# Block-sparse attention and a SoLU feed-forward: mask rows written into K^T and Q^T, and solu centred before the second matmul

## The chip, the cores and the metric

The kernel runs on one core of one Trainium2 chip. The metric is device time in microseconds (us) of one execution. A core has five engines with a queue each: TensorE (PE; its weight loads are PEld), VectorE (DVE), ScalarE (ACT), GpSimd (POOL) and SyncE (SP), which here only issues DMAs. Sixteen DMA engines serve all queues.

## What is computed

```python
# q, k, v: [4, 8, 768, 64];  blocks of 32, 24 of them, 3 sampled per row of blocks
scores = q @ k.T / sqrt(64)
mask = |blk_i - blk_j| <= 1, or block 0 or 23 on either side, or blk_j sampled for blk_i
attn = softmax(where(mask, scores, -1e9)) @ v
x = attn with the 8 heads side by side            # [3072, 512]
h = x @ w_in                                      # [3072, 1024]
solu = h * softmax(h)
ln = (solu - mean(solu)) / sqrt(var(solu) + 1e-6) * g_ln
out = ln @ w_out                                  # [3072, 512]
```

## The kernel before

**Units.** The work is cut into four batches. A batch has four pairs of heads and three tiles `t` of 256 queries. `prepare` brings K and Q of a pair into the forms kT and qT, with the 64 values of a head on the partitions and 768 tokens along the row; `attend` does one pair and one tile; `feed` does one tile of 256 tokens of the feed-forward in two halves of 128 tokens, so there are 48 calls of `attend` and 24 halves of feed.

**The mask.** The mask is part of the score matmul. Below the 64 rows of a head, kT has 24 rows that tell the block of each key, and qT has 24 rows that hold a large negative number for each block the query may not see. A score matmul therefore contracts over 88 rows. Before the change, these 24 values are put beside the 64 of each token in `kb` and `qb` (L356 to L365), and go through the transposes with them: `oneh` is built on POOL (L323), transposed on PE into `selq` (L329, L333), multiplied with `maskq` (L343, L348), and the product is copied to the three `qb` buffers (L365).

**Batch 0** is transposed on TensorE: a cast to bf16 (L441, L443), twelve transposes of 128x128 for the two heads of a pair (L458), one copy per head out of PSUM (L468, L470). **Batches 1 to 3** are cast on POOL (L417), transposed by a DMA (L422) and copied into kT and qT by DVE (L427); kT and qT have two buffers each, and the mask rows of the second are copied from the first by four DMAs (L643).

**attend.** Three steps of four score matmuls (L493), one exp each on ACT over 128x1024 (L500), then pv matmuls (L510) into one of two small PSUM banks (mbank), a reciprocal (L521) and the normalisation into x (L524).

**feed.** x is transposed by DMA (L554; the last tile on PE, L540). Per half: eight matmuls with w_in (L565), exp with its sum on ACT (L574), the product h * e on DVE (L577), the statistics (L580, L583), 1/sqrt on POOL (L585 to L590), a DMA transpose of the product (L598), eight matmuls with w_out (L605), the scaling (L615) and the store (L621). The mean is not subtracted from solu: w_out is centred instead. It is first scaled by g (L385), its column sums are formed on PE (L391) and brought to `wbar` (L396), and a second pass writes `w_out * g - wbar` (L398).

**Loads.** SP issues K, Q and V of the pairs in order, w_out (L379) and g (L382, one element per piece) after batch 0's, then the batches that follow. w_out in fp32 is held in the still unused parts of kT, qT and `eso` until it is scaled. w_in goes on POOL's queue (L375), since it is cast on the way, once the third V has landed.

**Order.** All instructions are first entered as operations with an engine, a duration, what they depend on, the buffers they take and a due time. `Plan.run` then places them: an engine takes, of what can start, the operation with the lowest due time. The due times of the units are in the tables A, F and Q, which are shifted by SHIFT. The order that comes out is fixed; each engine runs its own list in order and waits where something is late.

Of the kernel before, what the change touches and what calls it, by code (L numbers as in the profile page):

```python
# [7 lines left out]
FP32 = mybir.dt.float32  # L8
# [45 lines left out]
class Plan:  # L54
# [24 lines left out]
    def run(self):  # L79
# [10 lines left out]
        while len(order) < len(self.ops):  # L90
# [20 lines left out]
            if o.load is not None and o.xbar:  # L111
                self.xbar_free = max(self.xbar_free, t + 1.0) + o.load * (1.4 if self.dma_free > t + 1 else 1.0)
                self.dma_free = max(self.dma_free, t) + o.load
                o.seen = self.xbar_free + 1.3
            elif o.load is not None:
                self.dma_free = max(self.dma_free, t + 1.0) + o.load
                o.seen = self.dma_free + 1.3
                self.landed.append(self.dma_free)
                if len(self.landed) > 6 and o.eng == "SP":
                    self.free["SP"] = max(t + o.us, self.landed[-7])  # L120
# [20 lines left out]
def kernel(  # L141
# [14 lines left out]
    BLK = 32  # L156
# [47 lines left out]
    seb = bufs("se", [P, 1], FP32, 3)  # L204
    bnb = bufs("bn", [P, 2, 6], FP32, 3)
# [4 lines left out]
    wbar = const.tile([P, d_model], FP32, name="wbar")  # L210
# [10 lines left out]
    for nm, n in (("sh", 3), ("m", 2), ("kst", NST), ("qst", NST), ("vst", NST), ("kb", NKB), ("qb", NKB),  # L221
                  ("ex", NEX), ("x", NX), ("xT", NXT), ("e", NE), ("so", NSO), ("soT", NSOT), ("ot", NOT),
                  ("r", 2), ("se", 3), ("bn", 3), ("mv", 3), ("rs", 3), ("dq", 3)):
# [17 lines left out]
    def xbar_us(tiles):  # L241
# [7 lines left out]
        in_=bass.AP(tensor=_t32, offset=0, ap=[[2 * NR, NB], [1, 2 * NR]])), due=-100, load=0.01)  # L249
    warm = const.tile([1, 1], FP32, name="warm")  # L250
# [35 lines left out]

    def warm_mm(o):
        for _ in range(8):
            nc.tensor.matmul(bank(o)[:, 0:P], onesf, onesf, start=True, stop=True)

    for i in range(4):
        w = op("PE", 0.85, warm_mm, [m1], due=-60, take="m", after=[w] if i else [])
        w.last_of.append((w, "m"))
        w.held["m"][0] = 1


    oneh = const.tile([P, NCH, NB], BF16, name="oneh")
# [3 lines left out]
    kbf = const.tile([NB, NB], FP32, name="kbf")  # L301
    samp_f = const.tile([NB, NR], FP32, name="samp_f")
# [9 lines left out]
    def sel(t, us, fill, base, cm, pat, cmp=ALU.is_ge):  # L312
# [10 lines left out]
    ohs = chain(lambda o: nc.gpsimd.memset(oneh, 1.0),  # L323
                [sel(oneh, 0.3, 0.0, 0, NCH, [[1, NCH], [-BLK, NB]]),
                 sel(oneh, 0.3, 0.0, BLK - 1, -NCH, [[-1, NCH], [BLK, NB]])], -95)

    def selq_tr(o):
        for c in range(NCH):
            nc.tensor.matmul(bank(o, BF16)[0:NB, c * P : (c + 1) * P], oneh[:, c, :], ident, is_transpose=True,  # L329
                             start=(c == 0), stop=(c == NCH - 1))  # L330

    sqt = op("PE", 0.5, selq_tr, [ohs, mids], due=-88, take="m")
    sqs_ = op("DVE", dve_us(S, 2), lambda o: nc.vector.tensor_copy(  # L333
        out=selq.rearrange("b c p -> b (c p)"), in_=bank(sqt, BF16)[0:NB, 0:S]), [sqt], due=-88, last_of=[sqt])
    kbc = op("DVE", 0.2, lambda o: nc.vector.tensor_copy(out=kbf, in_=kbi), [io], due=-90)
    sf = op("DVE", 0.2, lambda o: nc.vector.tensor_copy(out=samp_f, in_=samp_i[:, :, 0]), [samp_dma], due=-90)
    last = op("DVE", 0.2, lambda o: nc.vector.tensor_scalar(  # L337
        out=anyeq, in0=kbf, scalar1=samp_f[:, 0:1], scalar2=None, op0=ALU.is_equal), [kbc, sf], due=-89)
    for r in range(1, NR):
        last = op("DVE", 0.2, lambda o, r=r: nc.vector.scalar_tensor_tensor(  # L340
            out=anyeq, in0=kbf, scalar=samp_f[:, r : r + 1], in1=anyeq, op0=ALU.is_equal, op1=ALU.max),
            [last], due=-89)
    mq = op("DVE", 0.2, lambda o: nc.vector.scalar_tensor_tensor(  # L343
        out=maskq, in0=anyeq, scalar=1.0, in1=static, op0=ALU.subtract, op1=ALU.mult), [last, stat], due=-88)

    def mask_mm(o):
        for c in range(NCH):
            nc.tensor.matmul(bank(o)[:, c * NB : (c + 1) * NB], selq[:, c, :], maskq, start=(c == 0),  # L348
                             stop=(c == NCH - 1))

    mmm = op("PE", 0.3, mask_mm, [mq, sqs_], due=-88, take="m")
    filled = {"k": [], "q": []}
    for i in range(NKB):
        for nm, t in (("k", kb), ("q", qb)):
            e = "DVE" if i == 0 else "POOL"
            z = op(e, 0.35, lambda o, t=t, i=i, e=e: (nc.vector if e == "DVE" else nc.gpsimd).memset(  # L356
                t[i][:, :, :, DM:].bitcast(I32), 0), due=-95 if i == 0 else -60,
                   after=[] if i == 0 else [mq])
            if nm == "k":
                f = op(e, 0.4, lambda o, i=i, e=e: (nc.vector if e == "DVE" else nc.gpsimd).tensor_copy(  # L360
                    out=kb[i][:, :, :, D:DM],
                    in_=oneh.rearrange("p (o c) b -> p o c b", o=1).broadcast_to([P, 2, NCH, NB])),
                    [ohs], due=-91 if i == 0 else -60)
            else:
                f = op("DVE", 0.4, lambda o, i=i: nc.vector.tensor_copy(  # L365
                    out=qb[i][:, :, :, D:DM],
                    in_=bank(mmm)[:, 0 : NCH * NB].rearrange("p (o c b) -> p o c b", o=1, c=NCH)
                    .broadcast_to([P, 2, NCH, NB])), [mmm], due=-87 if i == 0 else -39 + i,
# [326 lines left out]
```

## Time and profile before

| | |
|---|---|
| Time, median of 6 runs | 217.53 us (215.57 to 218.77) |
| The profiled execution | 217.16 us, its span 215.4 us |
| Granted TensorE clock, mean | 0.992 |
| PE busy | 201.1 us, 93% |
| ACT busy | 164.8 us, 77% |
| DVE busy | 148.8 us, 69% |
| POOL busy | 61.5 us, 29% |
| First score matmul | 8.66 us |
| Last exp of attention ends | 175.8 us |
| Last w_out matmul ends | 211.3 us |

The span runs from the first to the last instruction; the time of the execution has a little more around it. Busy shares are means over stretches with different limits, so they are read by stretch. A matmul counts as busy until its results are out, and matmuls overlap, so the work of TensorE is better counted in matmuls times the interval at which they follow each other.

### The profile page before, as it was taken

The page shows a single profiled execution, that of the slowest core. Times are in us where ns is not written, and L with a number is a line of the kernel's source. Part 1 is how long each engine was busy: PE and PEld are TensorE (multiplying, and loading weights), DVE is VectorE, ACT ScalarE, POOL GpSimd, SP SyncE. Part 2 cuts the span into 40 slices and gives each one's busy share as a digit, 9 for nine tenths or more (in the row PEclk, how much of TensorE's full clock was granted, in tenths as well). Part 3 has the DMA queues.
Part 4 walks back from the last instruction along what each step waited for, and adds up shares of the span by engine and source line. Part 5 has one row for each costly group of instructions (what it writes and reads, how often), then busy time and mean ns, then how long its engine had stood idle before and what let it go on. Part 6 is the DMA issues. An engine that isn't in the chain of part 4 may idle for free.

```text
span 215.4 us, 5758 instructions
## 1 busy us (share of the span) xinstructions
PE 201.1 (93%) x2284; PEld 141.7 (66%) x2284; DVE 148.8 (69%) x321; ACT 164.8 (77%) x198; POOL 61.5 (29%) x139
## 2 busy tenths in 40 slices
PE   7889977889999999999999999999999999999972
PEld 6667855567676688777777767777677764445530
DVE  7886554895886854467663867573858668999872
ACT  3489889389989899999999999899997982322300
POOL 7141014015154353132622241211301202231040
PEclk9999999699999999999999999999999999999999
DMA  5999999599999999999999998751312934968322
GB/s 182 324 378 335 248 283 174 165 214 254 216 303 190 245 239 241 249 282 213 328 147 281 225 296 212 144 138 36 97 48 53 114 85 115 215 147 187 122 102 97
DMA packets 73536, 42.66 MB, mean 198 GB/s; under 512 B 56420, under 2 KB 68708, under 8 KB 73508
## 3 DMA queue, kind: packets, MB, share of 16 engines
q1 hardware_dynamic: 72944, 41.24, 81.1%
q0 software_dynamic: 528, 1.05, 2.6%
q8 instruction: 18, 0.29, 0.6%
q14 instruction: 10, 0.08, 0.1%
q10 hardware_dynamic: 36, 0.00, 0.0%
HBM read 23.07 MB, written 6.29 MB: 136 GB/s over the span
## 4 chain that ended last, share of the span: by engine, by line
PE 75%; DMA 13%; DVE 5%; ACT 3%; issue 1%; POOL 1%; DVEq 0%; POOLq 0%; ACTq 0%
PE sbank L493 23%; PE mbank L605 18%; PE sbank L565 18%; PE mbank L510 13%; DMA kst<-in_k_dram 7%; ACT ex L500 3%; DMA kb<-kb 3%; DMA qb<-qb 2%; PE sbank L458 1%; DVE kT L470 1%; DVE anyeq L337 1%; DVE ot L615 1%; DVE eso L577 1%; PE mbank L540 0%; POOL kb L417 0%
## 5 line engine op out<-in xcount | busy, mean ns | idle before, releaser
L500 ACT ACTIVATE ex<-sbank 128x1024 bf16<-128x1024 f32 x144 | 137.7, 1034 | 10.9 <-PE sbank L493 9.1
L493 PE MATMUL sbank<-qT,kT 88*128 88x256 bf16 x576 | 85.5, 274 | 2.3 <-ACT ex L500 1.1
L493 PEld LDWEIGHTS <-kT 88*128 88x128 bf16 x576 | 53.2, 97 | 27.7 <-issue 5.1
L565 PE MATMUL sbank<-w_in_sb,xT 128*128 128x512 bf16 x192 | 52.6, 383 | 0.1
L510 PE MATMUL mbank<-va,ex 128*128 128x65 bf16 x1152 | 48.5, 194 | 2.6 <-DVE x L524 2.6
L510 PEld LDWEIGHTS <-ex 128*128 128x128 bf16 x1152 | 46.1, 98 | 7.3 <-issue 3.0
L605 PE MATMUL mbank<-w_out_sb,eso 128*128 128x512 bf16 x192 | 49.0, 379 | 1.1 <-DVE ot L615 1.1
L574 ACT ACTIVATE eso<-sbank 128x1024 bf16<-128x1024 f32 x24 | 24.9, 1036 | 21.9 <-issue 9.7
L577 DVE TENSOR_TENSOR eso<-sbank,eso 128x1024 bf16<-128x1024 f32 x24 | 29.2, 1217 | 6.6 <-ACT eso L574 6.2
L521 DVE RECIPROCAL r<-mbank 128x4 f32<-128x4 f32 x48 | 8.3, 176 | 34.7 <-PE mbank L510 34.5
L580 DVE BATCH_NORM_STATS2 bn<-eso 128x6 f32<-128x512 bf16 x48 | 30.6, 679 | 0.0
L605 PEld LDWEIGHTS <-eso 128*128 128x128 bf16 x192 | 17.7, 98 | 16.3 <-issue 1.2
L565 PEld LDWEIGHTS <-xT 128*128 128x128 bf16 x192 | 18.3, 99 | 11.5 <-issue 1.0
L587 POOL TENSOR_SCALAR mv<-se,mv 128x1 f32<-128x1 f32 x24 | 6.5, 272 | 64.3 <-DVE mv L583 57.6
L615 DVE TENSOR_SCALAR ot<-mbank,rs 128x512 f32<-128x512 f32 x24 | 17.8, 741 | 4.9 <-PE mbank L605 2.6
L476 POOL CAST va<-vst 128x768 bf16<-128x768 f32 x16 | 13.3, 832 | 26.5 <-PE mbank L510 14.4
L524 DVE TENSOR_TENSOR x<-mbank,r 128x256 bf16<-128x256 f32 x48 | 19.9, 419 | 1.0
L590 POOL TENSOR_TENSOR rs<-mv,neg_half 128x1 f32<-128x1 f32 x24 | 13.2, 549 | 5.9 <-DVE ot L615 4.2
L417 POOL CAST kb<-kst 128x768 bf16<-128x768 f32 x12 | 9.9, 824 | 14.0 <-DMA kst<-in_k_dram 14.0
L585 POOL TENSOR_TENSOR se<-se 128x1 f32<-128x1 f32 x24 | 4.7, 197 | 28.7 <-ACT eso L574 28.6
L417 POOL CAST qb<-qst 128x768 bf16<-128x768 f32 x12 | 10.2, 848 | 8.2 <-DMA qst<-in_q_dram 6.7
L427 DVE COPY kT<-kb 64x768 bf16<-64x768 bf16 x24 | 8.8, 366 | 5.1 <-DMA kb<-kb 4.8
(67 smaller groups left out, 90.0 us busy)
## 6 DMA issues: line engine op xcount, KB each, us to landing
vst<-in_v_dram SPq DMA_DIRECT2D x16, 384.0 KB, 5.1
out_dram<-ot SPq DMA_DIRECT2D x24, 256.0 KB, 2.9
kst<-in_k_dram SPq DMA_DIRECT2D x15, 384.0 KB, 5.6
qst<-in_q_dram SPq DMA_DIRECT2D x15, 384.0 KB, 4.9
w_in_sb<-in_moe_w_in_dram POOLq DMA_DIRECT2D x1, 1024.0 KB, 13.4
kT<-in_moe_w_out_dram SPq DMA_DIRECT2D x1, 768.0 KB
qT<-in_moe_w_out_dram SPq DMA_DIRECT2D x1, 768.0 KB
eso<-in_moe_w_out_dram SPq DMA_DIRECT2D x1, 512.0 KB, 16.9
```

Source lines behind the costliest of these rows:

```text
L417: nc.gpsimd.tensor_copy(out=half(cb[o.slot], 0).rearrange("p (c h d) -> p c h d", c=NCH, h=2), in_=st[ld.slot].rearrange("p h c d -> p c h ...
L476: vc = op("POOL", pool_us(S) + 0.3, lambda o: nc.gpsimd.tensor_copy(out=va[i][:, 2 * pr : 2 * pr + 2, :, 0:D], in_=vst[ld.slot]), [ld, von ...
L493: nc.tensor.matmul(s[:, m, :], kT[i][0:DM, pr, hh, jc * P : (jc + 1) * P], qT[i][0:DM, pr, hh, t * TW : (t + 1) * TW], start=(m % 2 == 0), ...
L500: exs.append(op("ACT", act_us(1024), lambda o, so=so: nc.scalar.activation(out=exb[o.slot], in_=sbank[so.slot], func=ACT.Exp, scale=scale) ...
L510: nc.tensor.matmul(acc[:, qt, hh, :], exb[exs[n].slot][:, m, qt * P : (qt + 1) * P], va[i][:, 2 * pr + hh, jc, :], start=(n + m + qt == 0) ...
L524: nrm = op("DVE", 0.39, lambda o: nc.vector.tensor_tensor(out=xb[x_of[(b, t)].slot][:, :, 2 * pr * D : (2 * pr + 2) * D].rearrange("p a (h ...
L565: nc.tensor.matmul(h[:, f * 512 : (f + 1) * 512], xTb[xp.slot][:, a, c, :], w_in_sb[:, c, f * 512 : (f + 1) * 512], start=(c == 0), stop=( ...
L574: se = op("ACT", act_us(d_ff) + 0.22, lambda o, h0=h0: nc.scalar.activation(out=eb[o.slots["e"]], in_=pair(h0), func=ACT.Exp, accum_out=se ...
L577: so = op("DVE", 1.19, lambda o, h0=h0, se=se: nc.vector.tensor_mul(out=sob[o.slot], in0=pair(h0), in1=eb[se.slots["e"]]), [se], due=F[a] ...
L580: bn = op("DVE", 2 * 0.64, lambda o, so=so: [nc.vector.bn_stats(out=bnb[o.slot][:, f], in_=sob[so.slot][:, f * 512 : (f + 1) * 512]) for f ...
L605: nc.tensor.matmul(bank(o0 or o), sotb[st.slot][:, f, :], w_out_sb[:, f, :], start=(f == 0), stop=(f == KF - 1))
L615: nc.vector.tensor_scalar(out=otb[o.slot], in0=bank(o0), scalar1=rsb[rs.slot], scalar2=None, op0=ALU.mult)
```

## The change

It does five things.

1. **Mask rows.** `selq` is built directly on POOL with 24 partitions and 768 columns. One PE operation of two matmuls forms the mask rows of Q for all 768 tokens. They are written to partitions 64 to 87 of kT and qT: for pair 0 by DVE and ACT, for the pairs 1 to 3 by one DMA each for kT and qT on POOL's queue, which repeats the rows of pair 0. `kb` and `qb` hold no mask columns any more. Batch 1's copies of the rows (the DMAs of L643) wait for the rows alone and no longer for pair 0's finished K^T and Q^T.
2. **Batch-0 transposes.** In pairs 1 to 3 both heads of a pair stand side by side, 128 columns, so six transposes serve two heads; they go to the small banks (`m`) instead of the score banks. In pair 0 each head keeps its own six, of 64 columns.
3. **Centring.** h * e also gives its sum over the row (`mu`); a new DVE instruction rewrites the product in place as `1024 * product - sum`. The statistics, the transpose and the matmul with w_out then use this, and eps is scaled by 1024 squared. The column sums, `wbar` and the second pass over w_out fall away.
4. **g** is loaded by ACT's queue as 8 rows of 128 and turned by one small matmul.
5. **w_in** is issued once the third K has landed, with a due time ahead of everything on POOL.

The planner's model of a DMA on POOL's queue is new, the four blocks of eight warming matmuls become seven of four, and the tables A, F, Q and SHIFT have new numbers, so the order of all the work differs.

```diff
-    ohs = chain(lambda o: nc.gpsimd.memset(oneh, 1.0), ...
-    sqt = op("PE", 0.5, selq_tr, [ohs, mids], due=-88, take="m")
+    sqs = chain(lambda o: nc.gpsimd.memset(selq, 1.0),
+                [sel(selq, 1.05, 0.0, 0, -BLK, [[1, NCH], [NCH, P]]),
+                 sel(selq, 1.05, 0.0, BLK - 1, BLK, [[-1, NCH], [-NCH, P]])], -93)
...
     def mask_mm(o):
-        for c in range(NCH):
-            nc.tensor.matmul(bank(o)[:, c * NB : (c + 1) * NB], selq[:, c, :], maskq, start=(c == 0),
-                             stop=(c == NCH - 1))
+        for g in range(2):
+            nc.tensor.matmul(sbank[o.slot].rearrange("p a b -> p (a b)")[0:NB, g * 512 : g * 512 + S // 2], maskq,
+                             selq.rearrange("b c p -> b (c p)")[:, g * (S // 2) : (g + 1) * (S // 2)],
+                             start=True, stop=True)
...
+        rows["k"].append(op("DVE", 0.3, lambda o, hh=hh: nc.vector.tensor_copy(
+            out=kT[0][D:DM, 0, hh, :], in_=selq.rearrange("b c p -> b (c p)")), [sqs], due=-2087 if hh == 0 else -60))
...
+    rest = {nm: op("POOL", 0.84, lambda o, t=t: nc.gpsimd.dma_start(
+        out=t[0][D:DM, 1:NPR].rearrange("p a h q -> p a (h q)"),
+        in_=t[0][D:DM, 0:1].rearrange("p a h q -> p a (h q)").broadcast_to([NB, NPR - 1, 2 * S])),
+        rows[nm], due=-2059, load=0.8) for nm, t in (("k", kT), ("q", qT))}
...
     w_in_load = op("POOL", 0.82, lambda o: nc.gpsimd.dma_start(
-        out=w_in_sb, in_=moe_w_in.rearrange("(c p) f -> p c f", p=P)), [stage[("v", 0, 2)]], due=-10, load=6.0)
+        out=w_in_sb, in_=moe_w_in.rearrange("(c p) f -> p c f", p=P)), [stage[("k", 0, 2)]], due=-2000, load=6.35)
...
-    g_load = op("SP", 0.45, lambda o: nc.sync.dma_start(
-        out=g_sb, in_=moe_g_ln.rearrange("(c p) -> p c", p=P)), due=-43.1, load=0.8, after=w_out_load)
+    g_load = op("ACT", 0.1, lambda o: nc.scalar.dma_start(
+        out=g8, in_=moe_g_ln.rearrange("(c p) -> c p", p=P)), due=-99.5, load=0.01)
+    gt = op("PE", 0.1, lambda o: nc.tensor.matmul(bank(o)[:, 0:KF], g8, identf[0:KF, 0:KF], start=True, stop=True),
+            [g_load, idf], due=-60, take="m")
...
-    wo = [op("DVE", 0.66, lambda o, c=c: nc.vector.scalar_tensor_tensor(
-        out=w_out_sb[:, c, :], in0=w_out_f[c], scalar=g_sb[:, c : c + 1],
-        in1=wbar, op0=ALU.mult, op1=ALU.subtract), [wb], due=28) for c in range(KF)]
+    wo = [op("DVE", 0.39, lambda o, c=c: nc.vector.tensor_scalar(
+        out=w_out_sb[:, c, :], in0=w_out_f[c], scalar1=g_sb[:, c : c + 1], scalar2=None,
+        op0=ALU.mult), [w_out_load[c // 3], gc], due=26) for c in range(KF)]
...
-            so = op("DVE", 1.19, lambda o, h0=h0, se=se: nc.vector.tensor_mul(
-                out=sob[o.slot], in0=pair(h0), in1=eb[se.slots["e"]]), [se], due=F[a] + 3, take="so",
+            so = op("DVE", 1.29, lambda o, h0=h0, se=se: nc.vector.scalar_tensor_tensor(
+                out=sob[o.slot], in0=pair(h0), scalar=1.0, in1=eb[se.slots["e"]], op0=ALU.mult,
+                op1=ALU.mult, accum_out=mub[o.slots["mu"]]), [se], due=F[a] + 3, take=("so", "mu"),
+            ce = op("DVE", 0.35, lambda o, so=so: nc.vector.tensor_scalar(
+                out=sob[so.slot], in0=sob[so.slot], scalar1=float(d_ff), scalar2=mub[so.slots["mu"]],
+                op0=ALU.mult, op1=ALU.subtract), [so], due=F[a] + 3, last_of=[(so, "mu")])
...
-    SHIFT = {"score": -851.13, "hmm": -451.93, "outp": 381.49, "pv": -264.97}
+    SHIFT = {"score": 17.85, "hmm": -42.86, "outp": 468.14, "pv": 80.68}
```

## The prediction

> **What bounds the kernel now.** I read the page's busy shares and slices first, then the chain that ended last, then a table by stretches, then the timeline where the table shows a loss.
>
> ```profile
> PE 201.1 (93%) x2284; PEld 141.7 (66%) x2284; DVE 148.8 (69%) x321; ACT 164.8 (77%) x198; POOL 61.5 (29%) x139
> PEclk9999999699999999999999999999999999999999
> PE 75%; DMA 13%; DVE 5%; ACT 3%; issue 1%; POOL 1%; DVEq 0%; POOLq 0%; ACTq 0%
> ```
>
> TensorE sets the end, but one slice has a low clock (the 6), and 13% of the chain are transfers, all early. The stretches:
>
> ```profile
> 0.00:8.60 8.60, 6.21 (x68) 5.23 (x69) 6.90 (x20) 2.51 (x4) 5.08 (x27) 1.00 0.73 219
> 8.60:24.00 15.40, 13.86 (x209) 12.17 (x209) 9.51 (x22) 14.02 (x16) 3.50 (x4) 1.00 1.07 346
> 24.00:36.30 12.30, 10.66 (x148) 8.07 (x145) 8.00 (x19) 10.69 (x12) 2.63 (x3) 1.00 1.17 221
> 36.30:48.00 11.70, 8.56 (x99) 6.21 (x99) 9.98 (x19) 7.29 (x10) 1.78 (x3) 0.85 0.85 199
> 48.00:177.40 129.40, 129.01 (x1600) 94.63 (x1598) 84.02 (x197) 122.30 (x144) 40.03 (x77) 1.00 0.88 194
> 177.40:212.20 34.80, 32.77 (x169) 15.35 (x167) 30.35 (x48) 8.00 (x16) 8.46 (x25) 1.00 0.54 138
> ```
>
> Columns: stretch, length, PE, PE loads, DVE, ACT, POOL busy, clock, DMA share, GB/s. Since a busy PE is not a full one, I price its work by the chain's pieces: score (L493) 0.44 us for 4, so 0.11; pv (L510) 0.75 for 24, so 0.031; feed (L565, L605) 0.86 for 4, so 0.215; a transpose of L458 0.83 for 12, so 0.069. From 48.0 to 206.0 the trace counts 448 scores, 920 pv, 184 + 177 feed matmuls: 49.3 + 28.8 + 77.6 = 155.7 us in 158.0. TensorE is full there, so whatever is gained or lost before 48 us moves the end by as much. From 36.3 to 48 it does 27 scores, 64 pv, 8 feeds = 6.7 us in 11.7: **5.0 us are lost**. Before that, exps pace it (ACT 14.02 of 15.4 and 10.69 of 12.3). The loss in the timeline:
>
> ```profile
> 37.24 0.79 DVE L427 COPY kT<-kb 64x768 bf16<-64x768 bf16 x2 [2.85 <-DMA kb<-kb]
> 38.15 0.42 DVE L524 TENSOR_TENSOR x<-mbank,r 128x256 bf16<-128x256 f32 x1
> 38.63 0.72 PE L510 MATMUL mbank<-va,ex 128*128 128x65 bf16 x16 [2.39 <-DVE x L524]
> 40.30 1.02 ACT L500 ACTIVATE ex<-sbank 128x1024 bf16<-128x1024 f32 x1 [2.94 <-PE sbank L493]
> ```
>
> VectorE stands in order behind a copy that waits for batch 1's first K transpose; the normalisation behind it holds a PSUM bank, TensorE waits 2.39 us, its granted clock then falls to half (L493 x4 takes 0.85 instead of 0.44, L565 x8 2.28 instead of 1.73). The x8 L398 passes (39.2 to 46.9) keep w_out unfinished, so no L605 runs before 54.
>
> **The change, part by part** (saving negative).
>
> *A. Mask rows and first score.* Now maskq is ready at 5.98, then six L348 matmuls, L365 0.45, transposes, L470 0.55, first score 8.66. After: two 384-column matmuls (0.16 each, by a feed's 512 columns at 0.215), about 0.2 of waits, an ACT copy like L468 (0.80), 0.1: 1.4 us behind the later of maskq and selq. selq is built on POOL: by the rows of 24 and 144 elements (memset 0.108 and 0.208, select 0.195 and 0.336) 768 elements cost 0.63 and twice 1.07, 2.8 us, against 3.0 us taken off POOL (oneh, its copies, zero fills). So it is ready at about 5 to 5.5, first score 6.6 to 7.4 on data that landed at 3.8. Bounds -2.0 and +0.5 (maskq held to 7.5); I take -1.2. DVE gains three row copies (0.37 each, by L427's 768 columns) and loses L333 1.12, three L365 of 0.45 and 0.75 of fills: hidden.
>
> *B. Batch-0 transposes and column sums.* Three pairs need 12 instead of 24 transposes: 36 x 0.069 = 2.5 us of PE. L391's 8 x 0.215 = 1.7 us and ACT's 0.60 go. But exps pace 8.6 to 36.3, and ACT is idle there only 3.0 us. Two of its gaps stand behind such work (0.98 before 25.72, 0.55 before 30.96). I take -1.0; bounds 0 and -3.0. The copies of 64 partitions still move 768 columns (0.55), free of cost against before. Transposes now take the two mbanks that pv uses; the freed score bank covers this, and if it doesn't, each collision costs one copy, 0.55, inside the bound of 0.
>
> *C. w_out in one pass.* L398 (5.8 us) and the wait for the whole column sum go; w_out is usable when L385's eight (0.48 each) are done, about 34 instead of 46.9. L605 and batch 1's later mask rows are released 12 us earlier, and DVE's order in 36 to 48 is empty enough that x isn't held. g's 1,024 pieces of 4 bytes leave the SP queue (landing 16.3 us, L385 waits 2.3 for it) for 8 rows on ACT's, 0.63 us of issue before the table load, hidden since q lands at 3.75; one small matmul and two DVE copies (0.2 each) bring g into place while w_out is on its way. What stays is that K of batch 1 comes through full DMA queues (share 1.07, 1.17), so I take -3.5 of the 5.0; bounds -5.0 and 0.
>
> *D. Queues.* The mask rows of three pairs become two POOL transfers of 216 KB. L643's like (96 packets of 3 KB) took 1.5 us of all engines; 144 take 2.2, g's give back 0.65, so w_out and K of batch 1 land 1.5 later. I hide this behind the 36 exps of batch 0 (36 x 0.94 = 34 us from 7.5, to 41); without that cover +1.5. On POOL, va's casts stand behind the rows' waits (to about 7.5); pv needs va at 13.2, so that is hidden. w_in's issue (14.71) moves to K of pair 2 (cast at 13.53), 1.2 us sooner; the 1 MB still ends with w_out near 28, first needed at 41. It costs nothing.
>
> POOL's transfers start late: w_in, issued by 15.69, shows its first packet at 19.15, 3.4 us later. The Trainium skill, SBUF — State Buffer, "SBUF: two separate sides", says that while a VectorE op in a two-port mode runs, GpSimd cannot write the descriptors of its DMAs, which speaks against sending rows this way in the stretch with most casts; it would put pair 1's rows behind two of VectorE's copies of 0.55 and make the sum 1.1 us worse, an estimate. By the trace alone rows issued at 7.5 to 8 land at 12 to 14, and pair 1 is needed after six exps, at 13.2: 0 to +1, I take 0.
>
> *E. Centring, 24 times on DVE.* L577 (1.217) becomes a scalar_tensor_tensor with a sum. L398's like takes 0.742 for 512, so 1.275 for 1,024; reading the sum out has no row on DVE, ACT's takes 0.212, so 0 to 0.21: +0.06 to +0.27, I take +0.18. The centring of 1,024 bf16: below, L427's copy of 768 (0.366) gives 0.43; above, L615's pace (0.741 for 512 from PSUM) gives 1.27; nearest is L385, 0.48. Together **+0.66 per tile** (0.49 to 1.54). In 48 to 177 DVE has 45 us free and takes 16 x 0.66 = 11: no cost. From 177.4 to 212.2 eight tiles run beside 30.35 busy in 34.8: 8 x 0.66 = 5.3 against 4.45 free, +0.85, and the last tiles' chain (exp, product, centring, transpose) is about 0.6 longer where TensorE already waits 1.11 for L615. I take **+2.0**; bounds +0.3 and 8 x 1.54 - 4.45 = +7.9.
>
> The Trainium skill, VectorE: DVE Perf Modes, "Two Vector instructions with no wait between them", has an op that writes out its accumulator as two instructions; no row of DVE here shows the second.
>
> **Sum:** -1.2 - 1.0 - 3.5 + 0 + 2.0 = -3.7 on a span of 215.4: 211.7. The profiled execution took 217.16, 1.8 around its span, and lies 0.37 below the median 217.53: predicted median 213.8.
>
> **Rivals.**
> 1. *The early gain is lost to DMA* (no change, 218.8): K of batch 1 (landing now at 30.1, then 6.0 of transpose) comes 1.5 later, TensorE waits for it as before, C is worth 0: -2.2 + 1.5 + 2.0 = +1.3. For it: the 13% of DMA in the chain. Against: only 28 exps had run by 37.4, so 8 of batch 0's 36 were left as cover.
> 2. *VectorE becomes the bound of the tail* (slower, 221.5): the centring takes L615's pace, +1.54 per tile, +7.9 at the end; against it stand A, B and, with VectorE behind from the start, half of C, -3.95: +3.95. Place: 177 to 212; it decides from (4.45 + 3.95 + 2.2) / 8 = 1.3 per tile, 2.2 being 1%. For it: DVE is 87% busy there. Against: L385's 0.48.
> 3. *The full early gain* (209.5): C -5.0, B -2.0, A -1.5, E +0.5 = -8.0.
>
> **Numbers.** Forecast 0.46, rival 1 0.22, rival 2 0.14, rival 3 0.18. A measurement here tells 1%, 2.2 us, from no change. Faster takes rival 3, nearly all of the forecast's 0.46 and a little of rival 1: 0.67; within 1% 0.19; slower 0.14. The range 209.0 to 219.0 holds all but rival 2's upper part and rival 3's edge; the forecast's own is 211.5 to 215.5.
>
> **What would show it.** Right: first score near 7.2; no half clock near 40; L605 before 48; PE full from about 40; a new bf16 line of 24 at 0.45 to 0.5; DVE above 95% from 177 on with TensorE gaps of 1 to 2 us. Wrong: the centring above 1 us, ACT waiting for pair 1's rows at 12 to 15, or batch 1's first score later than 39.

## The result and the profile after

The change made almost no difference: 217.47 us median (213.9 to 220.32, 40 runs) against 217.43 us for the kernel before in the same comparisons (82 runs). The ratio of the times is 0.9944, 95% interval 0.9919 to 0.9968; it counts of each kernel only the fast runs, those not over 1.5% above its fastest (12 of the kernel after), so it lies below the ratio of the two medians, and gains are given both ways where the two differ. The forecast was 213.8, a gain of 1.7%; by the ratio a third of that is there, by the medians nothing. The profiled execution took 217.81 us, its span 216.1, its clock 0.984.

The page of the kernel after, with the lines that answer to the first ones of before: busy time, clock, and the chain that ended last.

```profile
PE 198.5 (92%) x2228; PEld 138.8 (64%) x2228; DVE 152.7 (71%) x358; ACT 164.9 (76%) x198; POOL 63.2 (29%) x135
...
PEclk9996699999999999999999999999999999999999
...
PE 66%; DMA 15%; ACT 10%; DVE 4%; issue 1%; SPq 1%; POOL 1%; POOLq 0%; ACTq 0%; DVEq 0%
```

The low clock is no longer near 40 us: it has moved to the fourth and fifth slice, 16 to 27 us, and transfers still hold 15% of the chain. The stretches of the kernel after (length, busy time of PE, PEld, DVE, ACT, POOL, clock, DMA share, GB/s):

```profile
0.00:8.60 8.60, 6.55 (x63) 5.46 (x64) 5.94 (x17) 4.45 (x7) 5.54 (x22) 1.00 0.70 214
8.60:24.00 15.40, 9.29 (x96) 7.14 (x94) 7.61 (x16) 9.30 (x10) 3.68 (x5) 0.81 1.07 259
24.00:36.30 12.30, 11.26 (x179) 9.70 (x178) 9.38 (x23) 10.75 (x13) 1.66 (x2) 0.96 1.06 317
36.30:48.00 11.70, 10.15 (x148) 7.71 (x146) 2.95 (x10) 10.99 (x13) 2.48 (x3) 1.00 1.16 211
48.00:177.40 129.40, 127.16 (x1502) 90.24 (x1500) 96.17 (x232) 115.14 (x139) 42.71 (x83) 1.00 0.95 202
177.40:212.20 34.80, 34.05 (x253) 18.55 (x250) 30.01 (x62) 14.24 (x21) 7.11 (x21) 1.00 0.51 129
```

From 36.3 to 48 the loss of before is mostly gone: ScalarE is busy 10.99 instead of 7.29, at full clock. But 8.6 to 24 has become a hole: TensorE 9.29 busy instead of 13.86, ScalarE 9.30 instead of 14.02. The chain of waits of the kernel after through that hole (start, length, what):

```profile
2.66 5.63 DMA vst<-in_v_dram
8.28 0.06 issue
8.34 0.92 POOL va L454
9.26 10.15 DMA qT<-qT
19.42 0.14 issue
19.55 1.86 PE sbank L471 x8
```

POOL casts the first V (L454) as soon as it lands at 8.28; behind that cast stands the issue of Q's mask rows for the pairs 1 to 3 (L359, at 9.26); the 216 KB take 10.15 us to land; only then can TensorE score pair 1. The timeline shows the wait on both engines (idle time before the row, and who ended it):

```profile
20.60 1.94 ACT L478 ACTIVATE ex<-sbank 128x1024 bf16<-128x1024 f32 x2 [4.53 <-PE sbank L471]
```
```profile
19.55 1.86 PE L471 MATMUL sbank<-qT,kT 88*128 88x256 bf16 x8 [3.18 <-DMA qT<-qT]
```

At 18.05 the granted clock falls to half until 24.9: L471 x8 take 1.86 us here, where x11 took 1.63 at the start.

Where the time is won and lost is best seen in **work done**: all score, pv and feed matmuls that a trace shows up to a time, priced as in the prediction (0.11, 0.031 and 0.2155 us). I counted them in three traces, one execution each (217.16, 217.81 and 212.5 us); e3 is the experiment, told below, in which VectorE writes pair 1's rows.

| us of matmul work done by | 24 | 36.3 | 48 | 60 | 100 | 190 | span |
|---|---|---|---|---|---|---|---|
| before | 9.3 | 16.6 | 23.3 | 35.2 | 74.3 | 163.5 | 215.4 |
| after | 5.9 | 15.1 | 24.3 | 35.4 | 74.4 | 162.1 | 216.1 |
| e3_pair1_dve | 9.7 | 18.3 | 28.9 | 40.6 | 79.8 | 167.2 | 210.8 |

The kernel after is 3.4 us behind at 24, makes that good by 48, and stays within 1.4 of before from then on. With pair 1's rows on time (e3) it is 5.6 ahead at 48, and 4.6 shorter in the span.

### The profile page after: what moved, and what is told of

It is laid out like the page before. It is cut to its first block, busy times and chain, and to the rows that moved or that the text cites. A ratio compares the mean times of both kernels' runs of the same rounds, so it can differ in the third digit from the quotient of the medians.

```text
span 216.1 us, 5660 instructions
## 1 busy us (share of the span) xinstructions
PE 198.5 (92%) x2228; PEld 138.8 (64%) x2228; DVE 152.7 (71%) x358; ACT 164.9 (76%) x198; POOL 63.2 (29%) x135
## 4 chain that ended last, share of the span: by engine, by line
PE 66%; DMA 15%; ACT 10%; DVE 4%; issue 1%; SPq 1%; POOL 1%; POOLq 0%; ACTq 0%; DVEq 0%
PE sbank L471 21%; PE mbank L589 16%; PE sbank L543 16%; PE mbank L488 11%; ACT ex L478 10%; DMA vst<-in_v_dram 5%; DMA qT<-qT 5%; DMA kb<-kb 3%; DMA qb<-qb 2%; SPq L265 1%; PE mbank L518 1%; DVE kT L407 1%; PE mbank L437 1%; POOL va L454 1%; DVE bn L563 1%
## 5 line engine op out<-in xcount | busy, mean ns | idle before, releaser
L471 PE MATMUL sbank<-qT,kT 88*128 88x256 bf16 x576 | 85.9, 276 | 6.6 <-DMA qT<-qT 3.2
L471 PEld LDWEIGHTS <-kT 88*128 88x128 bf16 x576 | 53.5, 98 | 32.1 <-issue 10.3
L589 PE MATMUL mbank<-w_out_sb,eso 128*128 128x512 bf16 x192 | 48.0, 379 | 1.3 <-DMA eso<-eso 0.7
L488 PEld LDWEIGHTS <-ex 128*128 128x128 bf16 x1152 | 44.5, 98 | 5.8 <-DVE x L502 1.3
L488 PE MATMUL mbank<-va,ex 128*128 128x65 bf16 x1152 | 46.4, 194 | 0.7 <-DVE x L502 0.7
L552 ACT ACTIVATE eso<-sbank 128x1024 bf16<-128x1024 f32 x24 | 24.9, 1035 | 21.2 <-issue 11.4
L556 DVE SCALAR_TENSOR_TENSOR eso<-sbank,eso 128x1024 bf16<-128x1024 f32 x24 | 29.3, 1220 | 7.6 <-ACT eso L552 7.5
L543 PEld LDWEIGHTS <-xT 128*128 128x128 bf16 x192 | 18.0, 98 | 10.1
L454 POOL CAST va<-vst 128x768 bf16<-128x768 f32 x16 | 13.4, 835 | 20.2 <-DMA vst<-in_v_dram 20.2
L574 POOL TENSOR_TENSOR rs<-mv,neg_half 128x1 f32<-128x1 f32 x24 | 13.5, 564 | 12.9 <-DVE ot L599 11.7
L397 POOL CAST kb<-kst 128x768 bf16<-128x768 f32 x12 | 10.1, 839 | 8.1 <-DMA kst<-in_k_dram 8.1
L407 DVE COPY qT<-qb 64x768 bf16<-64x768 bf16 x24 | 9.9, 413 | 2.8 <-DMA qb<-qb 2.4
L560 DVE TENSOR_SCALAR eso<-eso,mu 128x1024 bf16<-128x1024 bf16 x24 | 11.6, 482 | 0.2
```

The source lines that it names most:

```text
L454: vc = op("POOL", pool_us(S) + 0.3, lambda o: nc.gpsimd.tensor_copy(out=va[i][:, 2 * pr : 2 * pr + 2, :, 0:D], in_=vst[ld.slot]), [ld, von ...
L471: nc.tensor.matmul(s[:, m, :], kT[i][0:DM, pr, hh, jc * P : (jc + 1) * P], qT[i][0:DM, pr, hh, t * TW : (t + 1) * TW], start=(m % 2 == 0), ...
L488: nc.tensor.matmul(acc[:, qt, hh, :], exb[exs[n].slot][:, m, qt * P : (qt + 1) * P], va[i][:, 2 * pr + hh, jc, :], start=(n + m + qt == 0) ...
L543: nc.tensor.matmul(h[:, f * 512 : (f + 1) * 512], xTb[xp.slot][:, a, c, :], w_in_sb[:, c, f * 512 : (f + 1) * 512], start=(c == 0), stop=( ...
L552: se = op("ACT", act_us(d_ff) + 0.22, lambda o, h0=h0: nc.scalar.activation(out=eb[o.slots["e"]], in_=pair(h0), func=ACT.Exp, accum_out=se ...
L556: so = op("DVE", 1.29, lambda o, h0=h0, se=se: nc.vector.scalar_tensor_tensor(out=sob[o.slot], in0=pair(h0), scalar=1.0, in1=eb[se.slots[" ...
```

## The experiments

In e1 to e5, e7 to e9 and c2 the order of each engine's list is that of the kernel after, and in c1 and d1 to d5 that of the kernel before, but for the instructions named; in b1, b2 and e6 the planner made a new one.

### The mask rows

**e1_rows_act and e2_rows_sp: the same transfers from another queue.**

```diff
-    rest = {nm: op("POOL", 0.84, lambda o, t=t: nc.gpsimd.dma_start(
+    rest = {nm: op("POOL", 0.84, lambda o, t=t: nc.scalar.dma_start(      # e2: nc.sync
```

> The changed kernel in its order, with the two transfers that repeat the mask rows for pairs 1 to 3 issued by ACT's queue instead of POOL's. Theory W (the late rows took the early gain): on POOL the Q rows are issued at 9.26 behind a V cast and land 10.2 us later; on ACT's queue they are issued near 8.7 and land in 3 to 5 us, the 3.2 us in which TensorE waits for them at 16.4 to 19.6 and the half clock after it go, and the time falls by 3 to 4.5 us against the changed kernel, to 213 to 214.5. Rival V (VectorE's centring eats the gain behind 48 us): the rows come early here too, but the time falls by less than 1 us. Rival Q (full DMA queues, whoever issues): the rows still land after 17 us and nothing changes.

> The same, with the two transfers on SP's queue, between the loads. W: they land about 5 us after their issue, behind some loads, at 13 to 14; the time falls by 2 to 4 us. V: less than 1 us. Q: they stand behind all loads issued before, land after 16, and the time falls by less than 1 us.

Both are slower: e1 221.44 us, ratio 1.0206 (1.016 to 1.0251), e2 225.17 us, ratio 1.036 (1.0304 to 1.0417). In e1 the issue itself is late: the exp ahead of it ended at 11.36, and it comes at 14.89. The trace puts these 3.53 us down to a load of K; what the issue waited for isn't shown. The rows land 7.42 us after it, at 22.30 (ScalarE's timeline, in which the issue has a row of its own, then the chain's piece):

```profile
14.89 0.79 ACTq L359 DMA_DIRECT2D qT<-qT  x1
15.72 4.69 ACT L478 ACTIVATE ex<-sbank 128x1024 bf16<-128x1024 f32 x5 [4.36 <-DMA kst<-in_k_dram]
```
```profile
14.89 7.42 DMA qT<-qT
```

In e2 the rows are issued at 10.95, behind the loads on SP's list, and TensorE waits four times as long as in the kernel after (the chain's piece, then TensorE's row in the timeline):

```profile
10.95 15.05 DMA qT<-qT
```
```profile
26.14 1.87 PE L471 MATMUL sbank<-qT,kT 88*128 88x256 bf16 x8 [12.40 <-DMA qT<-qT]
```

So from the other queues the rows come later, and the kernel is slower, which none of the theories in the expectations had. From issue to landing they take 7.42 us from ScalarE, 10.15 from POOL and 15.05 from SyncE: most of the delay is there without POOL's queue. Whether POOL adds the difference to ScalarE's 7.42 isn't shown. The prediction weighed the Trainium skill, SBUF — State Buffer, "SBUF: two separate sides", by which VectorE's work in a two-port mode could hold up descriptors that GpSimd writes. The rows from ScalarE and SyncE are not issued by GpSimd and took 7.42 and 15.05 us, so that rule isn't needed for most of the delay. What fits is the skill's DMA: Bandwidth & Descriptors, "Issuing engines are not separate DMA queues": transfers share the same 16 engines whoever starts them.

**e5_quiet_copy: the same transfer, once more, at a quiet time.** A copy of it into an unused tile is issued by POOL in front of a late L574.

```diff
+                if again:
+                    nc.gpsimd.dma_start(out=scr[D:DM]...,
+                        in_=qT[0][D:DM, 0:1]....broadcast_to([NB, NPR - 1, 2 * S]))
```

> The changed kernel, which in batch 3's first feed half issues the transfer of the Q rows a second time from POOL's queue, into a buffer that nobody reads, at a time when the DMA share is 0.2 to 0.5. Theory Q1 (the queue: the rows stand behind and between the loads of the full DMA engines): the same 216 KB land in 3 to 4 us here, against 10.2 at 9.26. Rival S (the transfer is slow by itself: 72 packets of 6 KB at 0.48 us, from POOL's descriptors): 7 to 10 us here as well.

The view of the DMA issues of this run (KB each, us from issue to landing), the early transfer and the late one:

```profile
qT<-qT POOLq DMA_DIRECT2D x1, 216.0 KB, 9.1
scr<-qT POOLq DMA_DIRECT2D x1, 216.0 KB, 4.1
```

The same bytes land in 4.1 us when they are issued at 176.6, where the DMA share is 0.72, and in 9.1 at about 9 us, where it is 1.07. VectorE is busy 4.21 of the 4.8 us around the late one and 5.31 of 10.1 around the early one, so VectorE's busy time doesn't explain the difference, and the load on the queues does. Three reservations: it is one execution; the share of 0.72 is above the 0.2 to 0.5 that was expected; and the two windows hold different VectorE instructions (the early one has four casts of 0.55 us, the late one mostly sums and statistics). The expectation's 72 packets of 6 KB would be twice the 216 KB that were moved.

**e3_pair1_dve: pair 1's rows by VectorE, the transfers only for the pairs 2 and 3.**

```diff
+        nc.vector.tensor_copy(out=t[0][D:DM, 1]..., in_=t[0][D:DM, 0]...)
         nc.gpsimd.dma_start(
-            out=t[0][D:DM, 1:NPR]..., in_=....broadcast_to([NB, NPR - 1, 2 * S]))
+            out=t[0][D:DM, 2:NPR]..., in_=....broadcast_to([NB, NPR - 2, 2 * S]))
```

> The changed kernel in its order; VectorE copies the mask rows of pair 1 itself (two copies of 24x1536, about 0.6 us each by the 0.35 of the 24x768 copy), and POOL's transfers bring only pairs 2 and 3. No transfer stands before pair 1. W: ACT's 4.5 us gap before 20.6 shrinks to under 1 us, the half clock goes, the time falls by 3 to 4.5 us. V: less than 1 us. Q: as W, since the transfers are out of pair 1's way.

212.75 us (212.5 to 214.97), ratio 0.9829 (0.9787 to 0.9871): this beats both kernels, the one after by 4.7 us (2.2%) in the medians and 1.2% in the ratios. It adds two copies of 0.61 to 0.64 us each, and its transfers carry a third fewer bytes. ScalarE runs 20 exps from 12.52 to 30.96 without a gap, and the stretch 8.6 to 24 is filled (the windows of e3, columns as above):

```profile
12.52 18.44 ACT L483 ACTIVATE ex<-sbank 128x1024 bf16<-128x1024 f32 x20 [0.47 <-PE sbank L476]
```
```profile
8.60:24.00 15.40, 14.57 (x180) 11.86 (x178) 12.80 (x27) 14.27 (x16) 3.18 (x5) 0.89 1.07 290
```

POOL's transfers still land 7.5 to 8.1 us after their issue, but nobody waits for them. The forecast of 213.8 is met as soon as pair 1's rows don't travel, though not by the parts that the forecast had (see below).

**e7_split: pair 1's rows as a transfer of their own, ahead of the others.**

> The changed kernel in its order; each of POOL's two row transfers is cut in two, pair 1 (72 KB) first, then pairs 2 and 3. Q1: the first packet still comes 3.5 to 4 us behind the issue and pair 1's rows of Q land at 14 to 16 instead of 19.4; TensorE's 3.2 us wait shrinks to under 1 and the time falls by 2 to 4 us against the changed kernel's 217.4. S: a third of the transfer takes a third of the 10.2 us, they land near 13 and the time falls as with VectorE's copies, by 4 to 5 us. If rows early don't matter: no change.

217.66 us, ratio 0.9964 (0.9917 to 1.001): no gain over the kernel after, where 2 to 5 us were expected. A third of the bytes (72 KB, issued at 9.28) still takes 7.3 us: size is the smaller part of the delay. TensorE no longer waits for qT, and at 24 us it is 2.5 us of work ahead of the kernel after (8.4 against 5.9), although this profile has the half clock from 7.3 to 17.6 us. Then it loses that lead at another load: the Q of pair 3, issued at 7.77, lands 16.86 us later (VectorE, then TensorE in the timeline of e7):

```profile
24.65 0.56 DVE L431 CAST qb<-qst 128x768 bf16<-128x768 f32 x1 [2.54 <-DMA qst<-in_q_dram]
```
```profile
26.30 0.49 PE L443 MATMUL mbank<-ident,qb 128*128 128x128 bf16 x6 [2.67 <-DVE kT L454]
```

At 36.3 it is 0.6 ahead, at 48 it is 0.5. In e3 the same Q is cast at 20.01 without a wait. So taking pair 1's wait away is not enough by itself here, and e3, which also sends fewer bytes, doesn't separate rows on time from lighter queues: how its gain divides between the two stays open.

**e8_warm: e3 with twice the warming matmuls (eight for four in each of seven groups).**

> e3_pair1_dve with eight in place of four warming matmuls in each of the seven groups before the first transposes, so TensorE is busy for about 1.5 us more before 7 us. If the half clock at 9.7 to 13.2 us of e3_pair1_dve comes from gaps in TensorE's work before it, the full clock holds through the first scores and the span falls by 0.5 to 1.5 us: 211.2 to 212.3 (ratio 0.971 to 0.977). Rival (the half clock comes whatever the warming, or the extra matmuls push the first transposes back): 212.5 to 214 (0.977 to 0.985).

215.99 us, ratio 0.9923 (0.9887 to 0.9959): 3.2 us worse than e3 by the medians, 2.0 by the ratios, and outside both expected ranges. The warming matmuls now end at 7.2 instead of 4.9, VectorE's work behind them (maskq) and the mask matmul come later, and the first score is at 11.22 instead of 8.70:

```profile
9.11 0.49 PE L343 MATMUL sbank<-selq,maskq 24*24 24x384 bf16 x2 [1.09 <-DVE maskq L337]
```

In this trace the half clock came all the same, from 9.6 to 16.4 instead of 9.7 to 13.2.

### The centring

**e4_no_centring and e9_e3_no_centring.** The product is taken without its sum and the centring instruction is not issued: solu is not centred in these two. e4 is this on the kernel after, e9 on e3.

```diff
-            so = ... nc.vector.scalar_tensor_tensor(out=sob..., in0=pair(h0), scalar=1.0, in1=eb..., accum_out=mub...)
+            so = ... nc.vector.tensor_mul(out=sob..., in0=pair(h0), in1=eb...)
-            ce = op("DVE", 0.35, lambda o, so=so: nc.vector.tensor_scalar(...), [so], ...)
+            ce = op("DVE", 0.35, lambda o: None, [so], ...)
```

> The changed kernel in its order, with the product formed without its sum and the centring left out (solu is not centred before w_out). It takes (0.083 + 0.482) x 24 = 13.6 us off VectorE. W: TensorE is full from 150 to 206 us in the changed kernel, so the time falls by 0.3 to 1.2 us, through the last half alone. V: it falls by 2 to 4 us.

> e3_pair1_dve in its own order with the centring left out as in e4_no_centring (24 x 0.57 us of VectorE fewer, the product without its sum). If the centring is free at the end, as in e4: 212 to 213.5 (ratio 0.976 to 0.982). If the prediction's term E holds where nothing else is lost, +2.0 for the centring: 210 to 211.3 (0.965 to 0.972).

The groups of the kernel after give the price of one (busy us, mean ns of one):

```profile
L556 DVE SCALAR_TENSOR_TENSOR eso<-sbank,eso 128x1024 bf16<-128x1024 f32 x24 | 29.3, 1220 | 7.6 <-ACT eso L552 7.5
...
L560 DVE TENSOR_SCALAR eso<-eso,mu 128x1024 bf16<-128x1024 bf16 x24 | 11.6, 482 | 0.2
...
L556 DVE DVE_READ_ACCUMULATOR eso<-sbank,eso 128x1 f32 x24 | 2.0, 83 | 0.0
```

Against 1.217 for the plain product that is 0.003 + 0.083 + 0.482 = 0.57 us per tile, 13.6 us of VectorE in all. Leaving them out brought nothing: e4 216.94 us, ratio 0.9996 (0.9959 to 1.0032), where the kernel after has 0.9944; e9 212.86 us, ratio 0.9789 (0.972 to 0.9859), where e3 has 212.75 and 0.9829. For e3 and e9 the medians say that the centring costs nothing, the ratios 0.9 us, and their intervals together leave up to about 2.6. The count of work says where it isn't: e9 is at most 0.6 us of work ahead of e3 up to 100 us, 1.8 at 112 and 1.7 at 200, so nothing is gained at the end. What is gained comes between 104 and 112, where e3's TensorE waits for `x` (0.7) and for a transposed `eso` (0.6) and e9's for nothing; one pair of traces doesn't show that the centring is the reason.

### w_out in one pass, and the loss at 36 to 48 us

**c1_before_one_pass: the kernel before without the second pass.** Column sums, wbar and L398 are not issued; w_out is scaled by g only, and nothing is centred.

```diff
-        o = op("PE", 0.216, lambda o, c=c, cs0=cs0: nc.tensor.matmul(...onesf, w_out_sb[:, c, :]...), ...
+        o = op("PE", 0.216, lambda o: None, ...                 # likewise wb and wo
```

> The kernel before in its own order, with w_out scaled by g alone: the eight column-sum matmuls (L391, 3.0 us of TensorE), ScalarE's wbar (L396) and VectorE's second pass over w_out (L398, 8 x 0.74 = 5.9 us) are left out, so w_out isn't centred and nothing else is put in its place. Nothing is re-planned. The prediction's term C: the stretch 36 to 48 us gets back most of its lost time, 214.0 to 215.5 (ratio 0.982 to 0.991). Rival (the stretch 36 to 48 is late for another reason, the transposed loads of batch 1 or the half clock at 39 us): 216.9 to 218 (0.997 to 1.002).

218.6 us, ratio 1.0063 (1.003 to 1.0097): the eight column sums (1.7 us of TensorE by the price above) and 5.9 us of VectorE less, and no gain; the time lies above the rival's range too. VectorE's timeline in c1:

```profile
33.58 0.42 DVE L521 TENSOR_TENSOR x<-mbank,r 128x256 bf16<-128x256 f32 x1
38.68 0.76 DVE L424 COPY kT<-kb 64x768 bf16<-64x768 bf16 x2 [4.68 <-DMA kb<-kb]
...
39.57 0.42 DVE L521 TENSOR_TENSOR x<-mbank,r 128x256 bf16<-128x256 f32 x1
```

VectorE comes to the copy of batch 1's first K with nothing else to do and stands there 4.68 us, where the kernel before stood 2.85; the normalisation behind the copy runs at 39.57, before at 38.15. The second pass runs behind this copy (39.2 to 46.9 before), and without it the next two normalisations still take 3.06 us from start to start, 3.27 before. But c1 doesn't price the pass alone: in its trace the transpose of that K took 7.87 us instead of 6.04, and the half clock lasted 6.8 us instead of 3.4; why isn't shown. Its runs show that the edit as a whole gains nothing.

**c2_second_pass: e3 with the second pass put back** as one block behind the last scaling of w_out (eight column sums, wbar, eight VectorE operations).

```diff
+            if len(wdone) == KF and 0 in users:
+                second_pass(mbank[users.index(0)])
```

> e3_pair1_dve with the cost of the second pass put back in full as one block behind the last scaling of w_out: eight column-sum matmuls, one ScalarE row, eight VectorE operations of about 0.74 us (5.9 us together). Nothing is re-planned, and since solu is centred already the second centring changes no result. If the pass was worth term C (-3.5), this loses 2 to 3.5 us against e3_pair1_dve: 214.8 to 216.2 (ratio 0.988 to 0.994). Rival (VectorE has room there, the pass was covered): 212.5 to 213.5 (0.977 to 0.982).

218.3 us, ratio 1.0054 (1.0017 to 1.0091): 5.5 us more than e3 by the medians, 4.9 by the ratios, above the expected 2 to 3.5. VectorE's timeline in c2:

```profile
34.34 3.21 DVE L396 SCALAR_TENSOR_TENSOR w_out_sb<-kT,g_sb,wbar 128x512 bf16<-128x512 f32 x3 [1.97 <-ACT wbar L394]
...
40.99 0.42 DVE L521 TENSOR_TENSOR x<-mbank,r 128x256 bf16<-128x256 f32 x1
```

Leaving the pass out of the order of before gained nothing; putting it into the order of after, as one block at a place that no planner chose, costs about 5 us. There the block holds the next normalisation from about 34 to 41, and by 48 us TensorE has done 132 scores and 240 pv instead of e3's 156 and 288. Part of that is not the pass: 12 of these 24 scores are missing already at 24 us.

**d1 to d5: what if batch 1's copy stands elsewhere?** d1 moves the four copies of batch 1's first K and Q behind the second pass on VectorE. d3 moves also the first half of feed 2.5 us later in the order. d5 is d3 with g loaded as in the kernel after. d2 and d4 are d1 and d3 without column sums, wbar and second pass (not centred).

```diff
+            if o in late:                       # d1: the copies L427 of batch 1, pair 0
+                held.append(o)
+                continue
+            if held and len(held) == len(late) and o.start >= first_use - 2.5:
+                for h in held:
+                    h.emit(h)
+        order.sort(key=lambda o: o.start + (2.5 if o in first_half else 0))      # d3
+                nc.tensor.matmul(t[:, 0:KF], g8, identf, start=True, stop=True)  # d5
```

> The kernel before, every instruction as it is and in its own order, but the four copies of batch 1's first pair (L427, for K and Q) stand later on VectorE: 2.5 us before the first score that uses them in the plan, behind the second pass over w_out in place of before it. If the place of the copy is what loses the time in 36 to 48 us, the normalisation goes ahead at about 34.5, TensorE's 2.4 us wait and ScalarE's 2.9 us gap go, the half clock at 39 us too, and the span falls by 2 to 4 us: 213.5 to 215.5 (ratio 0.982 to 0.991). If the second pass (5.9 us of VectorE) then stands in the way of the normalisations instead, 216 to 218 (0.993 to 1.002).

> d1_before_copy_later with the column sums, wbar and the second pass left out as in c1_before_one_pass (w_out is scaled by g, nothing is centred). If the copy's place is all, it is as d1 within 0.5%: 213.5 to 215.5. If the second pass has a price of its own once the copy is out of the way, it is 1.5 to 3.5 us faster than d1, 211 to 213.5 (ratio 0.970 to 0.982) with d1 near 216.

> d1_before_copy_later, and the first half of feed (its eight matmuls with w_in, exp, product, statistics and the transposing load) is entered 2.5 us later in the order of its engines, behind the scores and pv that stood after it. All work of the kernel before is kept. If the loss in 36 to 48 us is only the places ahead of late loads, TensorE's 2.4 us at L566 go and the span falls to 211.5 to 213: median 213.3 to 215 (ratio 0.981 to 0.989). Rival (the early time is given back later, or the next late load takes its place): 216.3 to 218 (0.995 to 1.002).

> d3_feed_later with the column sums, wbar and the second pass left out (w_out is scaled by g, nothing is centred). If the second pass costs nothing where VectorE does not stand in the way, as d3 within 0.5%. If it has a price of its own, 1.5 to 3 us faster than d3.

> d3_feed_later with g loaded as after the change: 8 rows of 128 on ScalarE's queue at the start, one small matmul and two small VectorE copies near 8 us, in place of 1,024 pieces of 4 bytes on SP's queue behind w_out. Else nothing differs; the second pass over w_out is kept. In d3 VectorE waits 2.9 us for g at 27 to 30, TensorE waits 1.9 us for the scaled w_out, and the second pair's K copies stand at 42 to 47. If g is the late load behind the rest of term C, the waits at 27 to 32 go, the second pass comes 2 us earlier, and the median is 212.5 to 214.8 (ratio 0.978 to 0.989). Rival (the next transposing load, at 42 to 47, is late by itself): 216 to 217.5 (0.994 to 1.001).

| run | us | ratio | 95% |
|---|---|---|---|
| d1 | 217.68 | 0.9997 | 0.996 to 1.0033 |
| d2 | 216.75 | 0.9953 | 0.9912 to 0.9995 |
| d3 | 216.81 | 0.9987 | 0.9958 to 1.0016 |
| d4 | 216.91 | 0.9989 | 0.9956 to 1.0023 |
| d5 | 217.21 | 1.0019 | 0.9974 to 1.0065 |

Each edit takes its wait away, and none gains 1%. In d1 the 2.85 us of VectorE are gone, and TensorE comes to the first feed matmul before its transposed x (TensorE in the timeline of d1):

```profile
40.56 1.90 PE L566 MATMUL sbank<-w_in_sb,xT 128*128 128x512 bf16 x8 [2.39 <-DMA xT<-x]
```

In d5 that wait and the one for g are gone too, and VectorE waits for the transposed Q of batch 1 at 58.85 and 69.71 (VectorE in the timeline of d5):

```profile
58.85 1.25 DVE L430 COPY qT<-qb 64x768 bf16<-64x768 bf16 x2 [0.83 <-DMA qb<-qb]
...
69.71 1.34 DVE L430 COPY qT<-qb 64x768 bf16<-64x768 bf16 x2 [1.36 <-DMA qb<-qb]
```

By the count of work d1, d3 and d5 are 1.2 to 1.4 us ahead of before at 48, and d3 and d5 only 0.1 and 0.3 at 80 (54.4 and 54.6 against 54.3). The kernel before has waits at these same two places, at 59.71 and 70.41. What d3 and d5 win by 48 they wait for again at batch 1's transposing loads. d1's trace keeps 1.3 at 80 and 0.9 at 100, but its runs show no gain. d2 against d1 and d4 against d3 leave no clear price for the second pass either.

### New orders

b1_centring_alone is the kernel before with the centring alone; b2_rows_without_centring is e3 with the centring undone and the second pass back; e6_replanned is the kernel after with e3's copies in the plan, slower transfers in its model and 0.48 for the centring. All three were planned anew with tables that belong to another set of operations.

```diff
-    rest = {... NPR - 1 ..., rows[nm], due=-2059, load=0.8) ...                                   # e6
+    near = {nm: op("DVE", 0.62, lambda o, t=t: nc.vector.tensor_copy(...), rows[nm], due=-2058) ...
+    rest = {... NPR - 2 ..., rows[nm], due=-2059, load=4.0) ...
-                [so], due=F[a] + 4, take="bn", last_of=[so])                                     # b1 (b2: back)
+                [ce], due=F[a] + 4, take="bn", last_of=[so])
```

> The kernel before with only the centring of the change: the product with its sum, the centring, w_out in one pass; no column sums, no second pass. Mask rows, transposes, g and the tables as before; the planner orders the work anew. By the prediction's terms C (part) and E: w_out done near 36 instead of 46.9, the half clock near 40 perhaps gone: -2 to -3.5 before 48 us, +0 to +2 at the end, so 214 to 216.5. Rival (the gain of the version with VectorE's row copies comes from the rows alone): 217 or more.

> The version with VectorE's copies of pair 1's rows (212.75) with the centring undone: two passes over w_out, column sums on TensorE, no sum in the product; the planner orders the work anew with that version's tables. If the one pass over w_out carries the gain, as term C has it: 215 to 218. If the mask rows and the six-fold transposes carry it: 212 to 214.

> The kernel after planned anew with what the runs showed: VectorE copies pair 1's rows (0.62 us each, in the plan), the rows of pairs 2 and 3 land later in the plan's model (load 4.0 in place of 0.8), the centring counted at 0.48. If the order is near enough to the tables' own, 211.5 to 213.5 (ratio 0.972 to 0.982). Rival (an order that the due times were not made for costs more than the better model brings, as in the two re-planned kernels): 214 to 220.

225.7 us (ratio 1.0323, 1.0247 to 1.0398), 224.77 (1.0284, 1.0226 to 1.0343) and 228.3 (1.0492, 1.0426 to 1.0557). b2 and e6 lie outside both ranges expected of them, and b1 in its rival's for another reason. They say nothing of the parts, only of the tables. In e6, which has e3's operations, the work is spread thinner in the middle of the kernel (windows of e6):

```profile
100.00:150.00 50.00, 45.94 (x593) 34.38 (x600) 34.76 (x89) 46.19 (x55) 15.65 (x29) 1.00 0.81 180
```

TensorE is busy 45.94 of 50 us there, in e3 48.70. The three re-plans cost 3 to 5%, more than the 1.7% that the whole change was forecast to bring.

## Why the prediction was wrong, step by step

**D, the queues, is the step that failed.** "By the trace alone rows issued at 7.5 to 8 land at 12 to 14, and pair 1 is needed after six exps, at 13.2: 0 to +1, I take 0." Q's rows were issued at 9.26 and landed at 19.4. Two things were mis-sized. The issue: I let V's casts stand behind the rows, but POOL's list has the first V cast ahead of Q's rows, and V landed only at 8.28. That cost at most 0.6 us, since the second head's rows were ready at 8.62; and K's rows, issued at 5.69 ahead of that cast, took 9.3 us to land as well. The landing is the larger part: I added 3.4 us to a first packet and 1.5 to 2.2 us "of all engines", as if the transfer had the engines to itself. e5 shows that this is near at a quiet time (4.1 us); in the full queues of the start it was 9 to 10. Against e3 the cost is 3.8 us of work at 24 us (5.9 against 9.7), 4.6 at 48, and 4.7 us of the time by the medians, 2.5 by the ratios; how much of that is the rows' own wait and how much the load that their bytes put on the queues is open (e7). The text had named the sign itself, "ACT waiting for pair 1's rows at 12 to 15"; ScalarE ran dry at 16. Rival 1 had the right kind of cause, an early gain lost to DMA, but at another transfer.

**A was right for the first score.** It starts at 7.59, forecast near 7.2: 1.07 of the 1.2. In e3 it is gone again: there VectorE's copy of pair 1's rows (6.34 to 6.95) stands ahead of maskq, and the first score starts at 8.70, before at 8.66.

**B and C were right as a sum and wrong in the reason for C.** A, B and C were to be worth 5.7 by 48 us; e3 shows 5.6. By stretches it is 1.65 up to 36.3, where A and B had 2.2, and 3.9 from there to 48, where C had 3.5, so the close sum is partly luck. And in c1 leaving out the second pass over w_out and its column sums gains nothing in the order of before: VectorE's stand is at the transposing load of K, which the prediction itself had shown in a fence, and the normalisation is held by that copy, with or without the pass. What the traces show in place of this wait is the new order: the copy of batch 1's first K comes at 46.34 in the kernel after and at 41.06 in e3, is not waited for, and has normalisations ahead of it. The sign "L605 before 48" failed as well: w_out is ready at 35.5, but the first w_out matmul is at 56.7 (before 54.3). B was not tried by itself. How much of the lead at 48 is the new order and how much is room that the removed work leaves in it stays open: moving single instructions in the order of before (d1 to d5) does not give it, and re-planning part of the change loses more than it could show.

**E was mis-sized.** 0.57 us per tile instead of 0.66, inside its bounds; at the end 0 instead of +2.0 (a cost in the middle, up to about 2.6, isn't excluded). The assumption was the tail of before, with attention over at 175.8 and eight tiles to do. After, nine exps run later than 177.4, only seven tiles are left, VectorE is busy 30.01 of 34.8 (30.35 before), not above 95%, and TensorE's list of waits from 177.4 on is one line:

```profile
PE mbank L589 <- DVE eso L522: 0.5, 1, 0.5
```

Before, the same list had 1.1 us. Rival 2, the centring as the bound of the tail, falls with e4 and e9.

**The sum.** With D repaired, e3 is 4.3 us (1.7% by the ratio) faster than before, as forecast (-3.7, 1.7%); but the parts differ. The forecast was -1.2 (A), -1.0 (B), -3.5 (C), 0 (D) and +2.0 (E); the count of work has about 0 for A, -1.65 for the stretch of B, -3.9 for that of C, nothing at the end, and +1.0 lost between 48 us and the end, most of it between 100 and 150 (5.5 ahead at 100, 4.1 at 150). That the two sums are so close is in part luck.

## What to carry to other kernels

Price a transfer by the landing times of transfers issued in the same stretch, with its place in the issuing list, and not by its bytes: here the same 216 KB took 4.1 us or 10.2, and copying what is needed first with a compute engine, 0.6 us a copy, was worth 2.2% by the medians and 1.2% by the ratios. Where an engine stands at a late load, taking away the work behind it won nothing here (c1), and taking one wait away won only as much as the next late load allowed (d3, d5, e7); so ask what is late next before booking a gain. Parts of a change that was planned as a whole are better tried by leaving instructions out of its own order than by planning a mixture.

## What was not expected of the hardware

- A DMA issue in ScalarE's list can hold up its exps: in e1 the issue of a 216 KB transfer came 3.53 us after the exp ahead of it had ended, and the next exp 4.36 us after. What the issue waited for isn't shown.
- Half-clock spells of TensorE had lengths in steps of 3.4 us in these traces: 3.4 in before and e3, 6.8 in after and e8, 10.2 in e7, 13.7 in e1 and e2. In before, after and e2 they began in a hole of TensorE's work of more than 2 us or just behind it; in e3 and e8 there were only gaps of about 1 us ahead of them. But d1 had a stand of 2.39 us and no half clock, and e9 none at all, so what brings them stays open; more warming at the start did not prevent one in the one trace of e8.
- VectorE's sum over a row of 1,024 costs one extra instruction of 0.083 us, and the product itself is no slower for it (1.220 against 1.217).
